# Window attention and a SiLU FFN on one core: block products for the second FFN product from the third chunk on, and a new order of operations

## The chip, the cores and the metric

The kernel runs on one core of a Trainium2 chip. The metric is the device time of one execution in microseconds (us). An execution has five engines with their own instruction streams: TensorE (PE in the profile; its weight loads are PEld), VectorE (DVE), ScalarE (ACT), GpSimdE (POOL) and SyncE (SP), which issues the DMA transfers.

## The reference

Four sequences of 768 positions with 8 heads of 64 go through an attention with a window of 15 positions to either side, plus 24 block summaries (the maximum of 32 keys, the mean of 32 values). The result, 3072 tokens of 512 numbers, goes through an FFN with a SiLU gate.

```python
k_sum = k.reshape(B, H, nb, block, D).max(axis=3)
v_sum = v.reshape(B, H, nb, block, D).mean(axis=3)
scores_l = where(|i - j| < 16, scale * q @ k^T, -1e9)
scores_s = scale * q @ k_sum^T + log(block)
a = softmax([scores_l, scores_s])
x = (a @ [v, v_sum]) as (3072, 512)
h = x @ w_in                       # 512 -> 2048
out = (h * sigmoid(h)) @ w_out     # 2048 -> 512
```

## The kernel before

**Tiling.** The attention runs in 24 stages of 128 positions: scores on TensorE (`job_scores`), softmax on VectorE, ScalarE and GpSimdE (`job_a`), values (`job_c`), and the result as x (`job_x`, L756 and L757). Two stages fill one chunk of 256 tokens, and the FFN takes the 12 chunks in turn. Attention for chunk c + 2 is put among the FFN of chunk c; three x buffers stand in a ring.

**The FFN.** Its 2048 inner columns are 16 blocks of 128; a unit is a pair of blocks (chunk 0 also has two single ones), so a chunk has 8 units. Each unit has a first product (x by w_in, into a PSUM bank of 512 columns), the gate (tanh on ScalarE, then one VectorE operation, which makes t), and a second product that accumulates over the chunk's units in PSUM. Chunk 0 works in f32. From chunk 1 on every operand is a sum of a high and a low f16 half, and a product is three f16 passes: high by high, high by low, low by high.

**Two forms of the second product.** `job_f` (L839 on) splits t into two halves (L889, L890) and multiplies directly: for two blocks, two halves of the 256 rows and three passes, 12 matmuls of 512 columns (L874), into two banks; at the chunk's end two copies (L911, L912) scale them into the output. `job_fast` (L952 on) treats the unit as a 2 by 2 matrix of blocks by another, and forms seven block products instead of eight (Winograd's form of Strassen's method): it splits three blocks of t (L969, L970), makes four sums of blocks in three subtractions on GpSimdE or VectorE (L974; the first is twice as wide), splits these (L976, L977), and issues seven products of three passes, 21 matmuls of 256 columns (L989), into four banks. At the chunk's end one copy and four VectorE additions (L1014, L1018, L1019) put the output together. The matching sums of w_out blocks are made once for each pair of blocks by `job_quad` (L929 to L934), ahead of the first use, and kept.

**What decides the form, and when the weight sums are made:**

```python
g, rest = divmod(i - FAST * NFT + EARLY, PACE)                            # L1161
if 0 <= g < NFT // 2 and not rest:                                        # L1162
    job_quad(g, n, FAST * NFT + 2 * g - TUNE["quad"])                     # L1163
(job_f if c < FAST else job_tail if c == NCHUNK - 1 and closes else job_fast)(n, c, fs)   # L1164
```

Here i counts blocks over all chunks (16 to a chunk, NFT = 16), and PACE is 4.

**The order of the work.** Every operation is recorded with its inputs, outputs and the engines that could run it (`Plan.op`). Two constants then settle the program: `RANKS` gives each operation a priority, and `ENGINES` a letter for its engine (P TensorE, D a DMA from SyncE, V VectorE, A ScalarE, G GpSimdE). A list scheduler (`Plan.sweep`, L124 on) takes the operations by them with assumed durations, and fixes each engine's own order; on the chip an engine follows its order and waits for its inputs. Where the scheduler foresees TensorE waiting in the first part, it puts fill matmuls on the identity (L310), whose result nobody reads.

**The start.** The first keys (`job_k0`), the first queries (`job_qk`), the values for the block means (`job_mean`) and the weights (`job_load`) come in as DMA transfers. The scores of the first two stages run in two halves each, the second when the third and fourth part of k have landed and been reduced. Three steps of eight matmuls (L522) sum the values for the means.

Of the kernel before, what the change touches and what calls it, by code (L numbers as in the profile page):

```python
# [56 lines left out]
FAST = 3  # L57
EARLY = 32
# [147 lines left out]
def local_attn_ffn(ctx: ExitStack, tc: tile.TileContext, qkT, qP, qF, kF, v, vR, vP, w, out):  # L206
# [1151 lines left out]
```

## Time and profile before

| | us |
|---|---|
| median of 3 runs | 570.09 (569.42 to 570.16) |
| the profiled execution | 570.2 |
| its span, first to last instruction | 568.5 |
| TensorE busy in it | 560.2 (99%) |
| VectorE busy | 483.1 (85%) |
| ScalarE busy | 391.8 (69%) |
| GpSimdE busy | 154.0 (27%) |

The profile is that of one execution. A busy time is the union of an engine's instructions. Matmuls overlap in their pipeline, so the time from one start to the next tells more of their cost than their own length. The stretches in the rows below follow the chunks roughly: chunk 0 runs from 22 to 86 us, chunk 1 from 86 to 131, chunk 2 from 131 to 179, with its last products up to 190, and then one chunk every 41 to 46 us.

### The profile page before, as it was taken

The numbers are of one execution on the slowest core, as the hardware profiler recorded it, in microseconds if no ns is written. First come the engines' busy times: TensorE is split into PE (matmuls) and PEld (weight loads), VectorE is DVE, ScalarE is ACT, GpSimd is POOL, SyncE is SP. The second block draws the span as 40 slices with busy tenths as digits, with TensorE's granted clock in tenths as the row PEclk, the third lists the DMA queues.
The fourth block names the chain that finished last, engine by engine and source line by source line (L and its number), as shares of the span: only waits on it lengthen the run. The fifth ranks groups of instructions, "written<-read, shape, count | busy, mean of one in ns | idle before, by whom it ended". The sixth has DMA issues, their size and how long they took to land.

```text
span 568.5 us, 16089 instructions
## 1 busy us (share of the span) xinstructions
PE 560.2 (99%) x6428; PEld 456.0 (80%) x6428; DVE 483.1 (85%) x1213; ACT 391.8 (69%) x995; POOL 154.0 (27%) x241
## 2 busy tenths in 40 slices
PE   8999999999999999999999999999999999999997
PEld 4767657676666888888888888888888888888885
DVE  6999989998999988998989877999988967834646
ACT  4999979767768975667878685758846766534431
POOL 4301000452523124232302212331323423323410
PEclk9999999999999999999999999999999999999999
DMA  8999733333895667346774567374871329200101
GB/s 331 414 419 414 283 107 103 99 109 107 187 230 103 186 163 92 122 119 209 195 184 144 161 122 93 134 132 106 236 190 48 85 57 65 75 1 3 38 1 37
DMA packets 66736, 83.92 MB, mean 148 GB/s; under 512 B 44950, under 2 KB 45350, under 8 KB 64870
## 3 DMA queue, kind: packets, MB, share of 16 engines
q1 hardware_dynamic: 66662, 82.91, 53.5%
q8 instruction: 50, 0.82, 0.6%
q14 instruction: 24, 0.20, 0.1%
HBM read 61.60 MB, written 11.16 MB: 128 GB/s over the span
## 4 chain that ended last, share of the span: by engine, by line
PE 83%; DMA 7%; ACT 5%; DVE 4%; issue 1%; SPq 0%; DVEq 0%; ACTq 0%
PE bank L949 30%; PE bank L989 26%; PE bank L861 7%; PE bank L874 7%; DMA wr<-in_w_dram 4%; PE bank L871 3%; PE bank L739 3%; PE bank L858 2%; PE bank L611 2%; DMA raw<-in_vR_dram 1%; ACT e L650 1%; ACT wr L786 1%; PE bank L724 1%; DMA first<-in_kF_dram 1%; ACT wr L782 1%; DMA raw<-in_qF_dram 1%
## 5 line engine op out<-in xcount | busy, mean ns | idle before, releaser
L949 PE MATMUL bank<-x,wr 128*128 128x256 f16 x1728 | 202.8, 273 | 0.0
L949 PEld LDWEIGHTS <-wr 128*128 128x128 f16 x1728 | 168.4, 98 | 20.2
L989 PE MATMUL bank<-wr 128*128 128x256 f16 x1491 | 177.2, 273 | 0.1
L974 POOL TENSOR_TENSOR wr<-wr 128x256 f32<-128x256 f32 (+1 forms) x139 | 95.2, 685 | 246.0 <-DVE wr L965 143.9
L989 PEld LDWEIGHTS <-wr 128*128 128x128 f16 x1491 | 144.1, 98 | 18.6 <-issue 0.3
L964 ACT ACTIVATE wr<-bank,th 128x512 f32<-128x512 f32 x71 | 48.5, 683 | 49.2 <-PE bank L949 48.8
L650 ACT ACTIVATE e<-e,mx 128x120 f32<-128x120 f32 x192 | 73.1, 382 | 10.9 <-DVE mx L647 10.9
L965 DVE SCALAR_TENSOR_TENSOR wr<-wr,bank 128x512 f32<-128x512 f32 x71 | 48.5, 683 | 27.6 <-ACT wr L964 27.2
L976 ACT ACTIVATE wr<-wr 128x512 f16<-128x512 f32 x71 | 44.3, 625 | 38.8 <-POOL wr L974 25.9
L977 DVE SCALAR_TENSOR_TENSOR wr<-wr 128x512 f16<-128x512 f32 x71 | 50.3, 709 | 17.3 <-ACT wr L976 17.0
L969 ACT ACTIVATE wr<-wr 128x384 f16<-128x384 f32 x71 | 36.9, 520 | 33.3 <-DVE wr L965 32.8
L970 DVE SCALAR_TENSOR_TENSOR wr<-wr 128x384 f16<-128x384 f32 x71 | 43.1, 607 | 6.2 <-ACT wr L969 5.2
L861 PE MATMUL bank<-x,wr 128*128 128x256 f16 x384 | 45.4, 273 | 0.0
L647 DVE CUSTOM_DVE_ANT_0 e<-bank,masks,qsc 128x120 f32<-128x120 f32 x144 | 42.4, 336 | 3.2 <-PE bank L611 3.0
L861 PEld LDWEIGHTS <-wr 128*128 128x128 f16 x384 | 37.1, 98 | 8.1 <-issue 0.3
L650 ACT ACTIVATION_READ_ACCUMULATOR e<-e,mx 128x1 f32 x192 | 36.1, 188 | 0.0
L929 POOL TENSOR_TENSOR wr<-wr 128x256 f32<-128x256 f32 x25 | 22.3, 901 | 35.5 <-DVE wr L934 10.3
L871 PE MATMUL bank<-wr,work 128*128 128x512 f32 x64 | 30.1, 597 | 0.1
L858 PE MATMUL bank<-x,wr 128*128 128x256 f32 (+1 forms) x144 | 30.1, 359 | 0.0
L858 PEld LDWEIGHTS bank<-x,wr 128*128 128x128 f32 x144 | 24.8, 190 | 5.3 <-issue 2.2
L665 POOL TENSOR_SCALAR e<-e,sum 128x120 f32<-128x120 f32 x26 | 10.4, 410 | 63.5 <-ACT e L650 31.9
L974 DVE TENSOR_TENSOR wr<-wr 128x128 f32<-128x128 f32 (+1 forms) x74 | 24.3, 328 | 2.4 <-POOL wr L974 1.7
(174 smaller groups left out, 798.6 us busy)
## 6 DMA issues: line engine op xcount, KB each, us to landing
wr<-in_w_dram SPq DMA_DIRECT2D x14, 1024.0 KB
raw<-in_qkT_dram SPq DMA_DIRECT2D x18, 576.0 KB
out_dram<-raw SPq DMA_DIRECT2D x23, 256.0 KB
first<-vd SPq DMA_DIRECT2D x30, 192.0 KB
raw<-in_kF_dram SPq DMA_DIRECT2D x12, 384.0 KB
raw<-in_qF_dram SPq DMA_DIRECT2D x9, 512.0 KB
raw<-in_vR_dram SPq DMA_DIRECT2D x12, 384.0 KB
raw<-in_vP_dram SPq DMA_DIRECT2D x9, 512.0 KB
```

Of the source, the lines that this page charges most:

```text
L650: plan.op({"act": 385}, lambda e, i=i, j=j, et=et, mx=mx: nc.scalar.activation(out=et[:, i, :], in_=et[:, i, :], func=AF.Exp, scale=-1.0, ...
L858: nc.tensor.matmul(out=o, lhsT=wi[:, ct * P:(ct + 1) * P], rhs=x0[:, ct, cs], start=(ct == 0), stop=(ct == NCT - 1))
L861: nc.tensor.matmul(out=o, lhsT=wip[:, part, ct * P:(ct + 1) * P], rhs=x[:, ct, :], start=(ct == 0 and q == 0), stop=(ct == NCT - 1 and q = ...
L871: nc.tensor.matmul(out=bank[ob[u]], lhsT=t[:, rows], rhs=wo, start=begins, stop=stops)
L949: nc.tensor.matmul(out=h[:, at * CH:at * CH + CH], lhsT=wip[:, p, ct * P:(ct + 1) * P], rhs=x[:, ct, :], start=(ct == 0 and q == 0), stop= ...
L964: plan.op({"act": 573}, lambda e: nc.scalar.activation(out=t, in_=h, func=AF.Tanh, scale=th[:, 0:1]), r=bk(k) + [("th", b % 2), "areas"], ...
L965: plan.op({"dve": 604}, lambda e: nc.vector.scalar_tensor_tensor(out=t, in0=t, scalar=1.0, in1=h, op0=ALU.add, op1=ALU.mult), r=bk(k), w=t ...
L970: plan.op({"dve": 470}, lambda e: nc.vector.scalar_tensor_tensor(out=ld, in0=src, scalar=SHRINK, in1=hd, op0=ALU.mult, op1=ALU.subtract), ...
L974: plan.op({"pool": 135 + 290 * size, "dve": 213 if size == 1 else 459}, lambda e, o=o, x=x, y=y: eng[e].tensor_tensor(out=o, in0=x, in1=y, ...
L976: plan.op({"act": 540}, lambda e: nc.scalar.activation(out=hs, in_=sf, func=AF.Copy, scale=SHRINK), r=[("sm", j)], w=[("hs", j)], prio=post)
L977: plan.op({"dve": 610}, lambda e: nc.vector.scalar_tensor_tensor(out=ls, in0=sf, scalar=SHRINK, in1=hs, op0=ALU.mult, op1=ALU.subtract), r ...
L989: nc.tensor.matmul(out=acc_of(c, m)[0], lhsT=x[:, left[m]], rhs=right[m](p), start=(opens and q == 0 and m in (1, 4, 2, 7)), stop=(closes ...
```

## The change

`FAST` goes from 3 to 2, so that chunk 2 too goes through `job_fast`. `EARLY` goes from 32 to 16, so that FAST * NFT - EARLY stays 16 and the weight sums are still recorded with blocks 16, 20 to 44. `RANKS` and `ENGINES` are replaced as a whole.

```diff
-FAST = 3
-EARLY = 32
+FAST = 2
+EARLY = 16
...
 RANKS = (
-    85, 28, 79, 25, 68, 114, 74, 106, 92, 65, 117, 138, 153, 163, 154, 335, 378, 544, 526, 132, 112, 19, 23, 2, 5, 3, 204, 216, 311, 465, 370, 425, 509, 607, 729, 599, 69,
...
+    (2792 priorities in place of 2760)
...
 ENGINES = (
-    "GDVDVDVDVDDDDDDDDDDPPPAVGAVGAGAGGAGAPPVAVAVAVAAVAVAGGGPPVVV
...
+    "GDVDVDVDVDDDDDDDDDDPPPAVGAGGGGVGGVAVPPVAVAVAVAAVAVGGAGPPVAV
...
```

The letters of the two strings, counted; "chunk 2's own" is what the new form itself adds:

| | P | V | A | G | D |
|---|---|---|---|---|---|
| before | 552 | 1011 | 726 | 233 | 238 |
| after | 540 | 1016 | 753 | 245 | 238 |
| difference | -12 | +5 | +27 | +12 | 0 |
| of which chunk 2's own | -12 | +21 | +8 | +15 | 0 |
| of which operations in both | 0 | -16 | +19 | -3 | 0 |
| of these, up to the end of chunk 2's list | 0 | -5 | +13 | -8 | 0 |

The engines of the three subtractions in chunk 2's eight units, in order: GGG, GVV, GVG, VVV, GGG, GGV, VVG, GVG.

Priorities of some of the first operations, a lower one first:

| operation | before | after |
|---|---|---|
| transfers of k, parts 0 to 3 | 28, 25, 114, 106 | 2, 1, 6, 15 |
| transfers of v for the means, 0 to 2 | 117, 138, 153 | 8, 35, 44 |
| scores, first halves of stages 0 and 1 | 69, 76 | 7, 9 |
| sums for the means, 0 to 2 | 132, 112, 19 | 24, 56, 72 |
| first transposes of stage 0 | 104, 93 | 51, 39 |
| scores, second halves of stages 0 and 1 | 118, 131 | 42, 45 |

## Rows read from the trace of the kernel before

**Rows 1.** The page, part 1: busy us (share) and instructions of each engine.
```profile
PE 560.2 (99%) x6428; PEld 456.0 (80%) x6428; DVE 483.1 (85%) x1213; ACT 391.8 (69%) x995; POOL 154.0 (27%) x241
```

**Rows 2.** Table of stretches: length, busy us (instructions) by engine, TensorE clock, DMA.
```profile
22.00:86.00 64.00, 62.97 (x379) 42.70 (x375) 59.92 (x128) 59.95 (x125) 5.39 (x10) 1.00 0.79 315
86.00:132.00 46.00, 46.00 (x488) 33.17 (x487) 44.54 (x104) 35.71 (x84) 16.67 (x26) 1.00 0.36 106
132.00:178.00 46.00, 46.00 (x526) 31.02 (x524) 42.78 (x110) 36.36 (x99) 16.83 (x18) 1.00 0.64 159
178.00:226.00 48.00, 48.00 (x625) 40.71 (x623) 42.21 (x119) 35.84 (x91) 13.66 (x21) 1.00 0.75 149
226.00:268.00 42.00, 42.00 (x504) 37.07 (x502) 40.47 (x97) 28.26 (x76) 11.16 (x18) 1.00 0.50 150
268.00:310.00 42.00, 42.00 (x546) 37.15 (x545) 37.94 (x99) 33.01 (x91) 8.48 (x12) 1.00 0.68 176
...
352.00:394.00 42.00, 41.88 (x543) 36.76 (x541) 41.30 (x113) 28.87 (x78) 12.06 (x17) 1.00 0.51 113
```

**Rows 3.** Timeline: start us, length us, engine, line, tiles, shape, count; TensorE, two places.
```profile
173.55 5.35 PE L874 MATMUL bank<-wr 128*128 128x512 f16 x24
...
178.74 2.78 PE L949 MATMUL bank<-x,wr 128*128 128x256 f16 x24
...
547.27 2.46 PE L989 MATMUL bank<-wr 128*128 128x256 f16 x21
...
549.56 1.47 PE L949 MATMUL bank<-x,wr 128*128 128x256 f16 x12
```

**Rows 4.** Groups by line and shape: count | busy us, mean ns of one | idle before.
```profile
L989 PEld LDWEIGHTS <-wr 128*128 128x128 f16 x1491 | 144.1, 98 | 18.6 <-issue 0.3
...
L977 DVE SCALAR_TENSOR_TENSOR wr<-wr 128x512 f16<-128x512 f32 x71 | 50.3, 709 | 17.3 <-ACT wr L976 17.0
...
L969 ACT ACTIVATE wr<-wr 128x384 f16<-128x384 f32 x71 | 36.9, 520 | 33.3 <-DVE wr L965 32.8
...
L970 DVE SCALAR_TENSOR_TENSOR wr<-wr 128x384 f16<-128x384 f32 x71 | 43.1, 607 | 6.2 <-ACT wr L969 5.2
...
L974 DVE TENSOR_TENSOR wr<-wr 128x128 f32<-128x128 f32 x51 | 14.6, 286 | 2.1 <-POOL wr L974 1.7
...
L1014 DVE SCALAR_TENSOR_TENSOR raw<-bank,th,wr 128x512 f32<-128x512 f32 x18 | 13.4, 744 | 2.1 <-PE bank L989 2.0
...
L974 DVE TENSOR_TENSOR wr<-wr 128x256 f32<-128x256 f32 x23 | 9.7, 420 | 0.3
...
L890 DVE SCALAR_TENSOR_TENSOR wr<-wr 128x512 f16<-128x512 f32 x8 | 6.4, 797 | 0.1
...
L784 DVE TENSOR_SCALAR wr<-wr 128x1024 uint32<-128x1024 uint32 x7 | 4.9, 695 | 0.0
...
L1014 DVE SCALAR_TENSOR_TENSOR raw<-bank,th,wr 128x256 f32<-128x256 f32 x9 | 4.3, 475 | 0.0
...
L912 DVE TENSOR_SCALAR raw<-bank,th 128x512 f32<-128x512 f32 x1 | 0.7, 745 | 0.0
```

**Rows 5.** Timeline, 168 to 200 us: x, block products, weight sums.
```profile
174.91 0.69 DVE L757 SCALAR_TENSOR_TENSOR x<-bank,x 128x512 f16<-128x512 f32 x1 [0.21 <-ACT x L756]
...
190.05 1.15 PE L989 MATMUL bank<-wr 128*128 128x256 f16 x9
...
195.09 1.28 DVE L934 SCALAR_TENSOR_TENSOR wr<-wr,ws 128x1024 f16<-128x1024 f32 x1
```

**Rows 6.** Timeline of TensorE, 0 to 53 us; in brackets its idle time and releaser.
```profile
6.85 0.40 PE L614 MATMUL bank<-first,second 64*64 64x96 f32 x8 [1.29 <-DMA second<-in_qP_dram]
...
8.26 2.55 PE L310 MATMUL bank<-ident 128*128 128x512 bf16 x11
...
12.06 1.06 PE L522 MATMUL bank<-wr,sums 128*32 128x512 f32 x8
...
41.21 0.40 PE L614 MATMUL bank<-first,second 64*64 64x96 f32 x8 [0.78 <-DMA second<-in_qP_dram]
```

More of the change, by code (lines that the diff above doesn't have):

```diff
@@ L1184 @@
 RANKS = (
[92 rows of a table removed]
[93 rows of a table added]
 )
 ENGINES = (
-    "GDVDVDVDVDDDDDDDDDDPPPAVGAVGAGAGGAGAPPVAVAVAVAAVAVAGGGPPVVVAVAVAVAVVVVGGGGPPVAPPPPAPPVAVAVAVAAVAVGGGGPPAVVAVAVAVAAVAVAGAGPPAVPPPPVDPVAVAVAVAAVGAAAPVAVAVAVAVAVVA"
-    "GGVPAAPVVVVPVPVVVVVVVAVDPVAVAVAVAVVAGAGPAAVAVAVAVAAVGVAVPAAPAVDAAVVDAVVADAVVVDAVVADAVVVADAVVVVDAAVVVDAVVVADAAVVVDAAVVADAVVVADAAVVVDAVVVADAAVVVDAAVVADAVVVADAVVVV"
-    "DAAVVAVPVPVVVVVVVVAVAVAVAVAVVVVVAVAVAVAVAVAVAVAVAVPPAVPPPPAVPPPPAVPPPPPPAVPPPPPPAVPPPPPPAVPPPPPPAVPPPPPPAVPPPPPPAVPPPPADADDPVAVAVAVAVVGAAGPAVVAVAVAVAVVGAAAPVVDD"
@@ L1284 @@
-    "VADVADVADVADADADAVVVDVVVVVVVPVAVAVAVAAVGAAGPAVVAVAVAVAAVGAAGPVAPAVPAVGGGGGGGGGGGAVVVDAVAVADVVDVVDVVDVVVVDVVVVVVVVAVDDGDVVDDAVDDDPVAVAVAVAVVVAVDDVAVAVAVAVVGVVDDD"
-    "AVAVGDDGGGGVAVPPAVAVPPPPPPAVAVPPPPGGGGAVPPAVAVPPPPPPAVAVPPPPGGGGAVPPAVAVPPPPPVAVAVAVAAVVAVDDVAVAVAVAAVGAVDDPAVPPAVAVPPPPGGGGAVPPAVAVPPPPPPAVAVPPPPADADDAVVVADAVD"
-    "DPVAVAVAVAAVAAVDDVAVAVAVAAVAAVDDPAVDAVAVADGGGVAVPPAVAVPPPPPPAVAVPPPPVGVGVVPPAVAVPPPPPPAVAVPPPPVVGVAVPPAVAVPPPPPVAVAVAVAVVVAVDDVAVAVAVAAVVAVDDPAVPPAVAVPPPPGGGGAV"
@@ L1287 @@
-    "PPAVAVPPPPPPAVAVPPPPADVDDAVAVADDVADVADVADVADADADAVVVDVVVVVVVPVAVAVAVAAVVAVDDVAVAVAVAVVVVVDDPAVDVVVVADPPAVAVGGGAVPPPPPPAVAVGGGAVPPPPAVAVVVGAVPPPPAVAVGVVAVPPPPAVA"
-    "VGVGAVPPPVAVAVAVAAVAAVDDVAVAVAVAAVGAVDDPAVPPAVAVGVGAVPPPPAVAVGGGAVPPPPAVAVGVGAVPPPPGVVVVVDDAVVVDVVAVVDVVDVVDVVDVVVVDVVVVVVVVAVDDDVVDDAVDDDPVAVAVAVAAVAAVDDVAVAVA"
-    "VAAVAVVDDPAVDAVAVADDPPAVAVGGGAVPPPPPPAVAVGVGAVPPPPAVAVVGGAVPPPPAVAVGGGAVPPPPAVAVGGGAVPPPVAVAVAVAAVAAVDDVAVAVAVAAVAAVDDPAVPPAVAVGGGAVPPPPAVAVVVVAVPPPPAVAVGGGAVPP"
@@ L1290 @@
-    "PPGAVVVVDDDAVAVVDAVDDPVAVAVAVAAVVVVDDVAVAVAVAVVGVVDDPAVDAVAVGDPPAVAVGGGAVPPPPPPAVAVVGVAVPPPPAVAVGGVAVPPPPAVAVGGVAVPPPPAVAVVVVAVPPPVAVAVAVAVVGAVDDVAVAVAVAAVVAVDD"
-    "PAVPPAVAVVVGAVPPPPAVAVVVVAVPPPPAVAVGVVAVPPPPGAVVVVDDDAVVVADDVADVADVADVADADADAVVVDVVVVVVVPVAVAVAVAAVVAVDDVAVAVAVAAVAAVDDPAVDAVAVGDPPAVAVGVGAVPPPPPPAVAVGGGAVPPPPA"
-    "VAVVVVAVPPPPAVAVVVVAVPPPPAVAVGGGAVPPPVAVAVAVAAVAAVDDVAVAVAVAAVGAVDDPAVPPAVAVVVGAVPPPPAVAVGGGAVPPPPAVAVVGVAVPPPPGAVVVVDDAVVVDVVVVADVVDVVDVVDVVVVDVVVVVVVVAVDDDAVD"
@@ L1293 @@
-    "DAVDDDPVAVAVAVAVVVAVDDVAVAVAVAAVAVVDDPAVDAVAVADDPPAVAVGGGAVPPPPPPAVAVGGVAVPPPPAVAVVGVAVPPPPAVAVGGVAVPPPPAVAVVGGAVPPPVAVAVAVAAVAVVDDVAVAVAVAAVVVVDDPAVPPAVAVGGGAV"
-    "PPPPAVAVGVGAVPPPPAVAVVVGAVPPPPGAVVVVDDDAVAVVDAVDDPVAVAVAVAAVVAVDDVAVAVAVAVVGAVDDPAVDAVVVGDPPAVAVGVVAVPPPPPPAVAVGGGAVPPPPAVAVGGGAVPPPPAVAVGVVAVPPPPAVAVGGGAVPPPVA"
-    "VAVAVAAVAVVDDVAVAVAVAAVAVVDDPAVPPAVAVVVVAVPPPPAVAVGVGAVPPPPAVAVVGGAVPPPPGVVVVVDDDVVAVADPVAVAVAVAAVVVVDDVAVAVAVAAVGAVDDPAVDAVAVGDPPAVAVGGVAVPPPPPPAVAVGGGAVPPPPAV"
@@ L1296 @@
-    "AVGGGAVPPPPAVAVVGGAVPPPPAVAVGVVAVPPPVAVAVAVAAVAVVDDVAVAVAVAAVAAVDDPAVPPAVAVVGGAVPPPPAVAVGGGAVPPPPAVAVGVVAVPPPPGVVVVVDDPAVPPAVAVVVGAVPPPPPPAVAVGGGAVPPPPAVAVGGVAV"
-    "PPPPAVAVGGGAVPPPPAVAVGGGAVPPPPAVAVVGGAVPPPPAVAVVGGAVPPPPAVAVGGGAVPPPPGAVVVVDDPPAVAVGGGAVPPPPPPAVAVGGGAVPPPPAVAVGGGAVPPPPAVAVVVVAVPPPPAVAVGGVAVPPPPAVAVGVVAVPPPPA"
-    "VAVVGVAVPPPPGVVVVVGPPAVAVAVAVPPPPPVDVDVD"
+    "GDVDVDVDVDDDDDDDDDDPPPAVGAGGGGVGGVAVPPVAVAVAVAAVAVGGAGPPVAVAVAVAVAVVAVVVGGPPAVPPPPAPPVAVAVAVAAVAVGGGGPPVAVAVAVAVAVVVVGGAGPPAAPPPPADPVAVAVAVAVVGGGAPVVVAVAVAVAAVA"
@@ new lines @@
+    "GGGPAAPVVVVPVPVVVVVVVAVDPVAVAVAVAVVGVAGPAVVAVAVAVAVVGAAAPVVPAVDAAVVDAAVADAAVVDAVVVDAVVVADAVVVADAVVVVDAAVVVDAAVVVDAAVVADAAVVADAAVVADAAVVADAVVVADAVVVADAAVVADAVVVA"
+    "DAAVVAVPVPVVVVVVVVAVAVAVAVVVAVAVAVAVVVAVVVAVAVAVAVPPAVPPPPAVPPPPAVPPPPPPAVPPPPPPAVPPPPPPAVPPPPPPAVPPPPPPAVPPPPPPAVPPPPADADDPVAVAVAVAAVAAGAPVVVAVAVAVAAVAAAAPAADD"
+    "VADVADVADVADADADAVVVDVVVVVVVPVAVAVAVAAVAAVAPAAVAVAVAVAAVAAAVPAAPAVPAVGGGGGGGVVVGAVVVDAVAVADVVDVVDVVDVVVVDVVVVVVVVAVDDGDVVDDAVDDDPVAVAVAVAAVAAVDDVAVAVAVAAVAAVDDD"
@@ new lines @@
+    "AVAVADDGGGGGAVPPAVAVPPPPPPAVAVPPPPGGGVAVPPAVAVPPPPPPAVAVPPPPGGVGAVPPAVAVPPPPPVAVAVAVAAVAAVDDVAVAVAVAAVAAVDDPAVPPAVAVPPPPGVGGAVPPAVAVPPPPPPAVAVPPPPADVDDAVAVGDAVD"
+    "DPVAVAVAVAAVAAVDDVAVAVAVAVVAAVDDPAVDAVAVADGVGGVVPPAVAVGGGAVPPPPPPAVAVGVVAVPPGVVVAVPPAVAVGVGAVPPPPAVAVVVVAVPPGGGGAVPPAVAVGGGAVPPPVAVAVAVAVVGAVDDVAVAVAVAAVAAVDDPA"
+    "VPPAVAVGGVAVPPGVVGAVPPAVAVVVGAVPPPPAVAVGVGAVPPPPGAVVVVDDDAVAVADDVADVADVADVADADADAVVVDVVVVVVVPVAVAVAVAVVAAVDDVAVAVAVAVVVAVDDPAVDAVVVGDPPAVAVGVGAVPPPPPPAVAVGGVAVP"
@@ new lines @@
+    "PPPAVAVGVGAVPPPPAVAVGGGAVPPPPAVAVGGVAVPPPVAVAVAVAAVAAVDDVAVAVAVAAVAAVDDPAVPPAVAVGVVAVPPPPAVAVGGGAVPPPPAVAVVGGAVPPPPGVVVVVDDAVVVDAVAVADVVDVVDVVDVVVVDVVVVVVVVAVDD"
+    "DAVDDVVDDDPVAVAVAVAAVAAVDDVAVAVAVAAVAAVDDPAVDAVAVADDPPAVAVGGGAVPPPPPPAVAVGGGAVPPPPAVAVGVVAVPPPPAVAVGVGAVPPPPAVAVGGGAVPPPVAVAVAVAAVAVVDDVAVAVAVAVVAAVDDPAVPPAVAVG"
+    "VGAVPPPPAVAVVGGAVPPPPAVAVGVGAVPPPPGAVVVVDDDAVAVVDAVDDPVAVAVAVAAVAVVDDVAVAVAVAVVGVVDDPAVDAVAVVDPPAVAVGGGAVPPPPPPAVAVGGGAVPPPPAVAVVGGAVPPPPAVAVGVGAVPPPPAVAVVVGAVP"
@@ new lines @@
+    "PPVAVAVAVAAVGVVDDVAVAVAVAVVVAVDDPAVPPAVAVGGGAVPPPPAVAVGGGAVPPPPAVAVVGGAVPPPPGAVVVVDDDAVAVGDDVADVADVADVADADADAVVVDVVVVVVVPVAVAVAVAAVAAVDDVAVAVAVAVVVAVDDPAVDAVVVG"
+    "DPPAVAVGGGAVPPPPPPAVAVVGGAVPPPPAVAVGVGAVPPPPAVAVGGGAVPPPPAVAVVGGAVPPPVAVAVAVAAVAAVDDVAVAVAVAAVAAVDDPAVPPAVAVVGVAVPPPPAVAVGVVAVPPPPAVAVGVGAVPPPPGAVVVVDDAVVVDAVAV"
+    "ADVVDVVDVVDVVVVDVVVVVVVVAVDDDAVDDAVDDDPVAVAVAVAAVAAVDDVAVAVAVAAVAAVDDPAVDAVAVADDPPAVAVGGGAVPPPPPPAVAVGGGAVPPPPAVAVVVVAVPPPPAVAVGGVAVPPPPAVAVGGVAVPPPVAVAVAVAAVVA"
@@ new lines @@
+    "VDDVAVAVAVAVVGAVDDPAVPPAVAVGGGAVPPPPAVAVGGVAVPPPPAVAVVVVAVPPPPGAVVVVDDDAVAVVDAVDDPVAVAVAVAAVGAVDDVAVAVAVAAVVAVDDPAVDVVAVGDPPAVAVGGGAVPPPPPPAVAVGGGAVPPPPAVAVGGVA"
+    "VPPPPAVAVGGVAVPPPPAVAVVGVAVPPPVAVAVAVAAVAAVDDVAVAVAVAAVGAVDDPAVPPAVAVGVVAVPPPPAVAVGVVAVPPPPAVAVGGVAVPPPPGAVVVVDDDVVAVVDPVAVAVAVAAVVVVDDVAVAVAVAAVVVVDDPAVDVVAVAD"
+    "PPAVAVVGGAVPPPPPPAVAVGGGAVPPPPAVAVVGGAVPPPPAVAVVGGAVPPPPAVAVGVGAVPPPVAVAVAVAVVVVVDDVAVAVAVAAVAVVDDPAVPPAVAVGVGAVPPPPAVAVGGGAVPPPPAVAVVGGAVPPPPGAVVVVDDPAVPPAVAVG"
@@ L1299 @@
+    "GGAVPPPPPPAVAVVGGAVPPPPAVAVVGVAVPPPPAVAVGGGAVPPPPAVAVVGGAVPPPPAVAVGGVAVPPPPAVAVGGGAVPPPPAVAVVGGAVPPPPGAVVVVDDPPAVAVGVVAVPPPPPPAVAVVGVAVPPPPAVAVVGGAVPPPPAVAVGGGA"
+    "VPPPPAVAVGGVAVPPPPAVAVVGVAVPPPPAVAVVVVAVPPPPGAVVVVGPPAVAVAVAVPPPPPVDVDVD"
 )
```

184 rows, old and new, of the table RANKS are left out of this document.

## The prediction

> **What bounds the kernel now.** I read the page's busy shares first, then the table of stretches, then the order of the matmuls. TensorE is busy for 560.2 of the 568.5 us span at a granted clock of 1.00, the upper level of 2.4 GHz [rows 1, 2]. The reader should not stop there, since a pipelined engine can look busy and be slow; so the start-to-start times matter. 24 matmuls of 512 columns take from 173.55 to 178.74, 216 ns each; 21 of 256 columns take from 547.27 to 549.56, 109 ns each [rows 3]. From 86 us on TensorE has no idle time to speak of: none in the five stretches to 310, 0.12 us from 352 to 394 [rows 2]. So there the kernel is as long as TensorE's list of work: work taken off it there is time won, as long as the other engines can still feed it.
>
> The engine to watch is VectorE. In the stretches 86 to 132, 132 to 178 and 178 to 226 it is busy for 44.54, 42.78 and 42.21 us, 129.53 of 140 [rows 2]. It has 10.5 us left there; ScalarE and GpSimdE have far more (9.6 and 29.2 us in 132 to 178 alone).
>
> **The change, part by part.**
>
> *Products (removed from the path).* A unit is a pair of FFN blocks. In chunk 2 a unit's second product is now 12 matmuls of 512 columns (two blocks, two halves of the rows, three half-precision passes), and becomes 21 of 256 (seven block products, three passes). By rows 3 that is 12 x 216 = 2.595 us against 21 x 109 = 2.290 us, 0.305 us less; eight units: **-2.44 us**. The first product (24 x 109 ns) is untouched. This term lies wholly on the path.
>
> The trace's row and a rule differ here. In the row, wide matmuls in a stream stand 216 ns apart [rows 3]. The Trainium skill, "TensorE: Matmul & The Clock Gate", section "Back-to-back issue gap", says that a sustained stream of weight loads and matmuls runs at about 131 ns per matmul of 512 columns and about 81 ns per matmul of 128. By that rule twelve wide ones would cost 1.57 us and 21 of 256 columns at least 1.70, and this term would be a loss of at least 1 us (rival E). The trace does not agree with the rule's 131 ns.
>
> *Block sums (added, beside the path).* For each unit VectorE now forms two low halves (607 and 709 ns) in place of one (797): +0.52 us, eight times 4.15 [rows 4]. The subtractions of a unit stand in the new engine string as GGG, GVV, GVG, VVV, GGG, GGV, VVG, GVG: two double ones (420 ns) and eight single ones (286) on VectorE, 3.13 us; six double and eight single ones go to GpSimdE, which is idle for most of that time [rows 2, 4]. Closing the chunk costs four additions (three of 744, one of 475) in place of one copy of 745: 1.96 us. **VectorE +9.2 us.** ScalarE gets one more copy of 384 columns per unit, 8 x 0.52 = 4.2 us, inside its 9.6 idle.
>
> *Shared weight sums (moved).* The eight "quad" jobs exist already and are issued beside the same units as before (48 - 32 = 32 - 16). But their user is now chunk 2, and the last one ends at 196.4 now [rows 5]. It has to be ready before the last unit of chunk 2, near 180. So the last two, with 1.28 us of VectorE each [rows 5] plus their sums, move forward by some 15 us; their total is unchanged.
>
> *Does VectorE still keep up?* The place that decides is the start of chunk 3. Its second half of x is written at 174.91 to 175.60, and its first matmul starts at 178.74: 3.1 us of lead [rows 3, 5]. By then VectorE must do most of the new work: 9.2 less the closing additions, 7.3, and about 2.6 for the two quads, so 9.9 us more. Cover: 4.7 us idle from 86 to 178 and 4.1 from 22 to 86 [rows 2]. The engine strings give the rest: among the operations that stand in both, 16 net leave VectorE, but only five of these belong to the parts up to the list of chunk 2; at between 0.29 (a block subtraction) and 0.70 us (a weight shift) each [rows 4], 1.4 to 3.5 us. 4.7 + 4.1 + 2.4 = 11.2 against 9.9: it fits, with nearly every idle slot used. An idle slot is not always usable, because each operation has its own inputs to wait for, so I book a stall of TensorE of **+0.5 us**, between 0 and 5.2 (9.9 - 4.7, if only the near idle time and no move helps). After 226 VectorE is 96 and 90% busy [rows 2], so what slips past chunk 3 is absorbed only slowly, but eleven of the sixteen operations leave it there.
>
> *Boundaries.* Accumulators: the seven products use four banks, and two of these hold chunk 1's sums until they are copied out. Today the same change of layout lies between chunks 2 and 3, the first block products start at 190.05 and TensorE has no gap around them [rows 2, 5]. Moved by a chunk it should cost nothing again; without that cover, one copy of 0.745 us [rows 4]. That sits in the bounds.
>
> *The new order (moved, everywhere).* From 86 us on there is no gap for it to close. Gaps and idle fills (matmuls on the identity that compute nothing) lie at the start: 11 fills from 8.26 to 10.74 while the second half of the first scores waits, and 0.78 us idle before 41.21 for a transfer of q; the first 6.85 us end with a transfer that nothing can pull forward [rows 6]. So at most 2.5 + 0.8 = 3.3 us are to be had. The new ranks move the first of the three sums for the block means, and one transpose, ahead of the second score halves, thus into the fills. Eight of the 24 matmuls of these sums, one such step, take 1.06 us [rows 6]. Against that, the last quarter of k is now issued behind the first transfer of v, so the second halves can come later. Bounds: 3.3 gained to 0.8 lost (one such wait as at 41.21). I take **-0.8 us**, a little under that row. The end has the same operations and is booked at nothing; it has no cover, and half a microsecond either way lies in the range.
>
> **Sum**, against the profiled execution of 570.2 us (span 568.5 and 1.7 around it): -2.44 + 0.5 - 0.8 = -2.7, so 567.5; the median of the runs is 0.1 lower, so **567.4 us**.
>
> **The rivals.**
>
> A. *VectorE is full, and slower.* One mechanism, at the start of chunk 3: if the operations moved off VectorE do not free it in time, 9.9 us of work meet 4.7 of idle time; x is 5.2 us late, and if the lead of 3.1 us is needed as it is now, TensorE waits all of it: -2.44 + 5.2 = +2.8, about 573. It turns slower once TensorE's waits exceed 2.4 us. For it: 97% busy in 86 to 132, 93% in 132 to 178. Against it: the engine string moves work away, and TensorE has products of older units to do while x is late (24 wide matmuls stood ready at 173.55 [rows 3]). Chance 0.07.
>
> B. *VectorE is nearly full, and the gain is eaten.* The lead is used up and 2.1 us (5.2 - 3.1) remain as waits, in one place or spread over the chunk: -2.44 + 2.1 = -0.3, about 569.8. Chance 0.14.
>
> C. *The start gains in full.* The fills and the wait for q vanish (-3.3) and nothing stalls: -5.7, 564.4; half of that start and no stall gives about 566. For it: the ranks of the first hundred operations are wholly new. Against it: the fills end on transfers and reductions that are still needed. Chance of 565.5 or below: 0.14.
>
> D. *The change does not do what it says*: the last quads come late, so that the last units' products wait and chunk 3's first products run first. TensorE would have chunk 3's first matmuls as filler, so the price is one quad's low half, 1.28 us [rows 5], and the time 568.7. Chance 0.06.
>
> E. *More and narrower matmuls cost more than they save.* Nine more matmuls per unit bring nine more weight loads of 98 ns [rows 4]. Were these not hidden behind the matmuls, a unit would grow by 9 x 98 - 305 = 577 ns, eight by 4.6 us: 574.5 with the other terms at nothing. Against it: the 109 ns of rows 3 hold with a weight load for each matmul. Chance 0.01. The rule of the Trainium skill named above ("Back-to-back issue gap") points the same way, to about 571.2.
>
> **How the numbers follow.** The forecast (565.5 to 568.6) has 0.58, C 0.14, D 0.06, B 0.14, A 0.07, E 0.01. About 0.2% (1.1 us) is what a measurement of this kernel can tell from no change. Faster by more than that, below 568.95: forecast, C and D, 0.78. Within it: B and a small part of A (0.01), 0.15. Slower, above 571.2: the rest of A and E, 0.07. The range reaches into C and B and leaves about one in ten out on either side: 565.2 to 569.9.
>
> **What would show it.** Right: 1659 block products (79 units x 21) and 96 wide matmuls; TensorE as good as without idle time from 86 us on; the first matmul of chunk 3 about 3 us earlier; VectorE at 97% or more between 86 and 226; fewer than 11 fills before the second score halves. Wrong: waits of TensorE's weight loads on VectorE's x or low halves between 130 and 230 (A, B), products waiting for the weight sums near 180 (D), or the second score halves starting later than 10.74 (the start lost).

## The result and the profile after

**Slower, not faster.** The median after the change is 576.3 us against 569.9 of the kernel before, run on the same chip: ratio 1.012 (1.010 to 1.014). I had forecast 567.4, with 569.9 as the upper end of the range. The execution profiled below took 576.5 us, its span is 574.4.

The table of stretches of the kernel after stands against [rows 2] (columns as there; the first number after the length is TensorE's busy time):

```profile
22.00:53.00 31.00, 31.00 (x249) 22.70 (x250) 30.05 (x85) 30.51 (x72) 4.54 (x10) 1.00 1.02 416
53.00:86.00 33.00, 31.86 (x163) 20.77 (x159) 32.29 (x52) 31.48 (x53) 1.35 (x3) 1.00 0.60 220
86.00:132.00 46.00, 45.15 (x451) 30.80 (x450) 43.01 (x99) 36.34 (x92) 15.28 (x21) 1.00 0.32 96
132.00:178.00 46.00, 44.22 (x596) 36.72 (x591) 42.69 (x123) 38.77 (x109) 15.48 (x21) 1.00 0.67 168
178.00:226.00 48.00, 48.00 (x640) 42.22 (x638) 42.67 (x110) 40.34 (x109) 17.46 (x22) 1.00 0.75 150
226.00:268.00 42.00, 41.67 (x501) 36.76 (x499) 40.02 (x106) 31.00 (x88) 12.64 (x18) 1.00 0.48 138
...
352.00:394.00 42.00, 39.85 (x468) 34.19 (x466) 36.04 (x95) 28.45 (x85) 9.73 (x16) 0.96 0.59 130
```

Before, TensorE had no idle time between 86 and 520 us but 0.12. Now it idles 0.85, 1.78, 0.33 and 2.15 us in four stretches, and 1.14 between 53 and 86. In the last row the mean granted clock is 0.96. The waits of TensorE's matmuls in the kernel after (line, what it waited for: us in total, times, longest):

```profile
PE bank L989 <- DVE wr L970: 2.2, 1, 2.2
PE bank L739 <- DMA first<-vd: 1.8, 2, 1.3
...
PE bank L522 <- DMA wr<-in_vP_dram: 0.8, 1, 0.8
PE bank L871 <- DVE wr L813: 0.7, 1, 0.7
```

These are not one place but many: a low half of the block products at 357 us, the values of window 6 at 160, the first values at 15, halves of the weights at 83. The groups by line and shape of the kernel after, against [rows 4], show that the products themselves arrived as meant, 79 units of 21 and 8 units of 12:

```profile
L989 PE MATMUL bank<-wr 128*128 128x256 f16 x1659 | 199.2, 273 | 2.5 <-DVE wr L970 2.2 <-DVE raw L1014 0.3
...
L874 PE MATMUL bank<-wr,work 128*128 128x512 f16 x96 | 22.7, 379 | 0.0
```

**The largest loss, followed back.** The timeline of TensorE in the kernel after:

```profile
355.25 0.38 PE L989 MATMUL bank<-wr 128*128 128x256 f16 x2
357.78 0.39 PE L989 MATMUL bank<-wr 128*128 128x256 f16 x1 [2.15 <-DVE wr L970]
357.97 5.24 PE L949 MATMUL bank<-x,wr 128*128 128x256 f16 x32
```

It waits 2.15 us for a low half of the block products. And the 32 matmuls behind the wait take 5.24 us. At the spacing of [rows 3] they would take 2.78 + 8 x 0.109 = 3.65. Right behind the idle time the granted clock is 0.50, the lower level of 1.2 GHz (columns as in the table of stretches), and that is another 1.6 us:

```profile
357.78:361.19 3.41, 3.41 (x17) 2.41 (x18) 3.41 (x18) 2.70 (x12) 0.45 (x1) 0.50 0.26 56
```

Not every execution has such a fall. Of the six, the three with a granted clock of 0.996 over the whole, this one among them, took 576.5 to 579.0 us, and the three with 0.999 to 1.000 took 575.8 to 576.1. So the loss stands without the fall too. What was the low half late for? VectorE's timeline there:

```profile
350.02 0.68 DVE L977 SCALAR_TENSOR_TENSOR wr<-wr 128x512 f16<-128x512 f32 x1
356.30 0.95 DVE L450 TENSOR_REDUCE am<-raw 128x1 f32<-128x768 f32 x1 [5.60 <-DMA raw<-in_vR_dram]
357.17 0.55 DVE L970 SCALAR_TENSOR_TENSOR wr<-wr 128x384 f16<-128x384 f32 x1
```

VectorE stood still for 5.6 us, because the next operation in its fixed order, a maximum over values of the fourth sequence (L450), waited for their transfer. The low half (L970) is queued behind it and needed nothing that was late. The issues of SyncE tell what the transfer stood behind:

```profile
343.32 0.88 SPq L580 DMA_DIRECT2D first<-vd  x2
344.30 5.05 SPq L706 DMA_TRANSPOSE third<-first  x2
349.52 0.47 SPq L447 DMA_DIRECT2D raw<-in_vR_dram  x1
```

The DMA row and the rate in GB/s for 340 to 358 us, in 40 slices of 0.45 us, of the kernel after:

```profile
DMA  8710000860957990909000000000990089990000
GB/s 328 193 24 0 0 0 0 164 128 9 218 205 167 127 32 23 28 28 32 27 23 27 27 23 27 27 23 18 288 78 3 10 271 328 295 215 0 0 0 0
```

From the 15th slice to the 28th, 346.3 to 352.6 us, only 18 to 32 GB/s move. The second transfer of L580 (158 KB: 79 rows of 2 KB, the second half of the values of a sequence's last window) trickles through. 158 KB at 25 GB/s are 6.3 us, the length of that trough. The trace's packet records show it: of the 175 packets of 2 KB of the two halves, 101 start between 344.49 and 346.34 us (as many as the 96 rows of the first half and five more), and the other 74 follow one at a time, one every 80 ns, until 352.28. What is issued meanwhile lands behind it: the load of L447 at 356.3, 6.8 us after its issue, where 3 to 3.5 are usual (one issued at 106.15 is read from 109.49 on). The Trainium skill, "DMA: Bandwidth & Descriptors", section "Why a DMA increments its semaphore by 16 and not by 1", has the rule: a copy is spread over the largest number of engines, up to 16, that divides its slowest dimension on both sides. 79 is prime, which by that rule leaves one engine, while 96 and 64 get 16. The trace agrees: 74 packets one at a time here, against 101 in 1.85 us just before. The kernel before has the same transfer and the same trough; VectorE's waits there, 340 to 356 us:

```profile
DVE am L450 <- DMA raw<-in_vR_dram: 2.7, 1, 2.7
```

There TensorE has no idle time between 310 and 352 us: nothing that it needed soon was queued behind L450.

### The profile page after: what moved, and what is told of

The parts are those of the page before. It is cut to its first block, busy times and chain, and to the rows that moved or that the text cites. A ratio compares the mean times of both kernels' runs of the same rounds, so it can differ in the third digit from the quotient of the medians.

```text
span 574.4 us, 16306 instructions
## 1 busy us (share of the span) xinstructions
PE 560.5 (98%) x6495; PEld 462.7 (81%) x6495; DVE 486.6 (85%) x1218; ACT 407.5 (71%) x1045; POOL 161.7 (28%) x252
## 4 chain that ended last, share of the span: by engine, by line
PE 73%; DMA 11%; DVE 9%; ACT 4%; issue 2%; SPq 1%; POOL 0%; DVEq 0%; ACTq 0%
PE bank L949 35%; PE bank L989 30%; DMA wr<-in_w_dram 5%; PE bank L739 3%; PE bank L611 2%; DMA raw<-in_vR_dram 2%; DMA wr<-in_vP_dram 2%; DMA raw<-in_qF_dram 2%; DVE wr L814 1%; DMA first<-vd 1%; DVE e L647 1%; ACT wr L812 1%; PE bank L874 1%; DVE wr L788 1%; DVE wr L934 1%
## 5 line engine op out<-in xcount | busy, mean ns | idle before, releaser
L989 PE MATMUL bank<-wr 128*128 128x256 f16 x1659 | 199.2, 273 | 2.5 <-DVE wr L970 2.2
L974 POOL TENSOR_TENSOR wr<-wr 128x128 f32<-128x128 f32 (+1 forms) x160 | 111.4, 696 | 289.4 <-DVE wr L965 157.3
L964 ACT ACTIVATE wr<-bank,th 128x512 f32<-128x512 f32 x79 | 53.7, 680 | 47.7 <-PE bank L949 47.4
L965 DVE SCALAR_TENSOR_TENSOR wr<-wr,bank 128x512 f32<-128x512 f32 x79 | 53.8, 681 | 31.1 <-ACT wr L964 30.6
L976 ACT ACTIVATE wr<-wr 128x512 f16<-128x512 f32 x79 | 49.3, 624 | 38.2 <-POOL wr L974 28.4
L977 DVE SCALAR_TENSOR_TENSOR wr<-wr 128x512 f16<-128x512 f32 x79 | 55.9, 708 | 12.9 <-ACT wr L976 12.4
L969 ACT ACTIVATE wr<-wr 128x384 f16<-128x384 f32 x79 | 41.0, 519 | 30.1 <-DVE wr L965 29.8
L970 DVE SCALAR_TENSOR_TENSOR wr<-wr 128x384 f16<-128x384 f32 x79 | 50.0, 633 | 10.4 <-ACT wr L969 9.7
L663 ACT ACTIVATE e<-e,sum 128x120 f32<-128x120 f32 x109 | 34.3, 383 | 0.6 <-DVE sum L658 0.6
L703 DVE TENSOR_TENSOR first<-e,first 128x480 f16<-128x480 f32 x36 | 24.9, 695 | 0.1
```

What stands on the lines that cost most here:

```text
L964: plan.op({"act": 573}, lambda e: nc.scalar.activation(out=t, in_=h, func=AF.Tanh, scale=th[:, 0:1]), r=bk(k) + [("th", b % 2), "areas"], ...
L965: plan.op({"dve": 604}, lambda e: nc.vector.scalar_tensor_tensor(out=t, in0=t, scalar=1.0, in1=h, op0=ALU.add, op1=ALU.mult), r=bk(k), w=t ...
L969: plan.op({"act": 430}, lambda e: nc.scalar.activation(out=hd, in_=src, func=AF.Copy, scale=SHRINK), r=tks, w=[("hd", j)], prio=post)
L970: plan.op({"dve": 470}, lambda e: nc.vector.scalar_tensor_tensor(out=ld, in0=src, scalar=SHRINK, in1=hd, op0=ALU.mult, op1=ALU.subtract), ...
L974: plan.op({"pool": 135 + 290 * size, "dve": 213 if size == 1 else 459}, lambda e, o=o, x=x, y=y: eng[e].tensor_tensor(out=o, in0=x, in1=y, ...
L976: plan.op({"act": 540}, lambda e: nc.scalar.activation(out=hs, in_=sf, func=AF.Copy, scale=SHRINK), r=[("sm", j)], w=[("hs", j)], prio=post)
```

## The experiments

Two theories at first. **Theory 1:** the new order, laid out for assumed durations, puts in-order engines behind transfers and sums that come later than planned. **Theory 2:** the block products in chunk 2 overfill VectorE.

| kernel | TensorE idle 0-53 | 53-132 | 132-178 | 178-268 | 352-394 | ratio to before (95%) |
|---|---|---|---|---|---|---|
| before | 4.13 | 0 | 0 | 0 | 0.12 | 1 |
| after | 3.72 | 1.99 | 1.78 | 0.33 | 2.15 | 1.012 (1.010 to 1.014) |
| order_alone | 4.42 | 1.25 | 0.14 | 1.45 | 2.53 | 1.012 (1.009 to 1.015) |
| products_alone | 3.11 | 2.41 | 0 | 2.51 | 0 | 1.005 (1.003 to 1.007) |
| after_split | 4.66 | 1.59 | 2.30 | 0 | 0 | 1.005 (1.003 to 1.007) |
| before_split | 4.05 | 0 | 0 | 0 | 0 | 1.000 (0.998 to 1.001) |
| after_light | 3.82 | 1.53 | 1.29 | 0 | 0 | 1.004 (1.002 to 1.005) |
| after_early6 | 4.54 | 1.42 | 1.78 | 1.36 | 0 | 1.007 (1.005 to 1.009) |
| told | 3.78 | 2.97 | 1.26 | 3.20 | 0 | 1.014 (1.010 to 1.017) |
| start_alone | 3.73 | 0.36 | 0 | 0 | 0.17 | 0.999 (0.998 to 1.001) |
| old_loads | 3.73 | 1.61 | 0.10 | 0 | 0 | 1.000 (0.999 to 1.001) |
| start_told | 4.74 | 2.13 | 0.45 | 0.46 | 0 | 1.003 (1.002 to 1.005) |
| loads_light | 3.89 | 1.01 | 0.10 | 0 | 0 | 0.999 (0.998 to 1.000) |
| before_light | 3.20 | 0 | 0 | 0 | 0.21 | 0.999 (0.998 to 1.000) |

Idle us are a stretch's length less TensorE's busy time in the one profiled execution, added up from tables of stretches like the one above; the ratios are over all executions.

**order_alone and products_alone: the two halves of the change, each by itself.** Constants: `FAST = 3`, `EARLY = 32` with the new `RANKS` and `ENGINES` of the operations that stand in both; and `FAST = 2`, `EARLY = 16` with the old ones. Neither is pure: order_alone's ranks were mended by hand between 125 and 400 us, so there its order is a new one, but not that of the changed kernel; and in the trace of products_alone VectorE's order is that of the kernel before only up to 60 us and after 282.

> The kernel before (chunk 2 by wide products) in the new order: every operation that stands in both kernels takes its place and its engine from the changed kernel; between 125 and 400 us ranks were mended by hand until the planner's own forecast had no hole (it forecasts 568.3 against 567.9 for the old order). Theory 1, the new order loses the time (in-order engines stand behind transfers and sums that come later than the planner assumed): slower than before by 3 to 8 us, 573 to 578, with waits of TensorE near 15, 54 to 90, 130, 160 and 350 us as in the changed kernel. Theory 2, the block products in chunk 2 lose it (VectorE is too full): 569.5 to 571, no new waits but those before 53 us.

> The changed kernel (chunk 2 by seven block products, weight sums 16 blocks earlier) in the old order: before 84 us and after 230 us ranks and engines of the kernel before, the new ones between, and there mended until the planner's forecast had no hole over 0.9 us (567.3 against 567.9 for before and 565.8 for the changed kernel). Theory 1 (the order): 568 to 571, the chunks from 4 on at their old distances, the products' 2.4 us partly to be seen. Theory 2 (the products): 574 to 577, like the changed kernel, with TensorE's waits between 86 and 230.

A new order alone cost 1.2%, as much as the whole change, without a single new block product (577.3 us). Theory 1 had forecast that, and theory 2 no change. Its waits are of the same kinds: between 70 and 90 us on the weights, at 239 and at 364. TensorE in order_alone:

```profile
237.27 0.82 PE L989 MATMUL bank<-wr 128*128 128x256 f16 x6
239.54 1.47 PE L989 MATMUL bank<-wr 128*128 128x256 f16 x12 [1.45 <-DVE raw L1014]
...
364.56 0.28 PE L989 MATMUL bank<-wr 128*128 128x256 f16 x1 [1.90 <-DVE wr L977]
```

Both of these can be followed back to a load that lands behind 79 rows, as in the changed kernel. VectorE waits for it and then works without a pause until TensorE's wait ends:

```profile
226.67 0.95 DVE L448 TENSOR_REDUCE vm<-raw 128x24 f32<-128x768 f32 x1 [3.20 <-DMA raw<-in_vR_dram]
...
357.97 0.95 DVE L450 TENSOR_REDUCE am<-raw 128x1 f32<-128x768 f32 x1 [4.82 <-DMA raw<-in_vR_dram]
```

The products in the mostly old order cost 0.5% (573.5), between the two forecasts. TensorE in products_alone:

```profile
84.74 1.55 PE L871 MATMUL bank<-wr,work 128*128 128x512 f32 x3 [1.40 <-ACT wr L812]
...
229.06 0.28 PE L989 MATMUL bank<-wr 128*128 128x256 f16 x1 [1.25 <-DVE wr L977]
...
234.48 0.49 PE L989 MATMUL bank<-wr 128*128 128x256 f16 x3 [1.21 <-DVE wr L1019]
```

The releasers are ScalarE once and VectorE twice, which looks like theory 2. But the two waits for VectorE, 2.5 us, can be followed back to the 79 rows once more:

```profile
227.38 0.95 DVE L448 TENSOR_REDUCE vm<-raw 128x24 f32<-128x768 f32 x1 [5.06 <-DMA raw<-in_vR_dram]
...
228.31 0.69 DVE L977 SCALAR_TENSOR_TENSOR wr<-wr 128x512 f16<-128x512 f32 x1
```

The load was issued at 218.20, while 79 rows were under way, and VectorE stood still for 5.06 us before it. It was not short of room; it was held up and then behind, without a pause until 234. What is left for theory 2 is the 1.4 us for a half of the weights at 84.74. No run divides the 79 rows in this kernel or in order_alone, so the price of the products in an order like the old one, and that of the order without the late transfers, were not measured.

**after_split and before_split: the 79 rows in two transfers.**

```diff
-                nc.sync.dma_start(out=vv[at:at + hi - lo, z], in_=vd_t[b - 1][lo:hi])
+                for r, q in ((lo, lo + HALF), (lo + HALF, hi)) if t == NTILE - 1 and z else ((lo, hi),):
+                    nc.sync.dma_start(out=vv[at + r - lo:at + q - lo, z], in_=vd_t[b - 1][r:q])
```

> The changed kernel with one thing taken away: the last window's second half of values, 79 rows of 2 KB, is loaded as 64 and 15 rows in two transfers (three times in the run). In the trace these 79 packets go one behind the other, one per 84 ns, and everything issued after them lands late (landings of 9.5 and 6.8 us where 3 to 4 are usual). If these 79 rows are what delays the load of values' sums at 349.5, and with it the low half and TensorE at 357.8: that load lands in 3 to 4 us, the 5.6 us wait of VectorE and the 2.3 us wait of TensorE go, and with them the 1.8 us of matmuls at half clock: 572.2 to 574. If the transposes ahead of it are what delays it: the landing stays above 6 us and the time at 576 +- 0.7.

> The same division of the 79-row transfer in the kernel before. There TensorE does not wait near 350, so the time should stay (569.5 to 570.5) while VectorE's 2.7 us wait near 350 goes and the transfers near 216, 342 and 470 land in 3 to 5 us. A gain of over 1 us would say that the late transfers cost the kernel before too.

573.2 instead of 576.3 us, in an unchanged order. In the profiled execution the late load now lands in 3.6 us, TensorE's wait at 357 and the fall of the clock behind it are gone (idle 0 in 352 to 394), and the trough with them: all 175 packets of the two halves pass between 344.57 and 346.52. Other executions still have a fall somewhere: five of ten, with a granted clock of 0.993 to 0.997 over the whole, took 573.6 to 575.7 us. The rate in after_split, same window and slices:

```profile
GB/s 348 217 31 0 0 0 0 119 171 1 73 328 282 105 133 195 9 144 131 10 7 0 116 82 273 371 262 61 0 0 0 0 0 0 0 18 84 55 266 375
```

That is shown, then: three transfers of 79 rows, together with the order that put a low half behind them, were 3 to 4 us of the loss (by medians and by ratios). The transposes ahead of the load, the rival, are still there, and TensorE waits for nothing behind them. In the kernel before the same division changes nothing: its order had no use for what it freed.

**after_light: less VectorE work in chunk 2.** In after_split, `part = slice(0, 16) if c == 2 and f > 5 else slice(None)` on both low halves (L970, L977).

> The changed kernel with the 79 rows in two transfers, where VectorE forms the two low halves of chunk 2's last five units on 16 columns only instead of 384 and 512 (the rest of these halves is left out), same order: some 4.5 us less for VectorE between 145 and 180, in the very sums that the change adds. Theory 2 (this work is what delays the rest): the wait of 2.4 us for values near 160 and what comes after it shrink, 569.5 to 571.5. Theory 1 (late transfers): VectorE idles more, the wait near 160 stays over 1.5 us, and the time stays at 572.5 to 573.8.

572.0 us; VectorE's busy time between 132 and 178 fell from 43.12 to 40.06 us, the idle time of TensorE there from 2.30 to 1.29. But in the changed kernel, whose order is the same up to there, that idle time was 1.78, so half a microsecond of the 1.0 can be chance. Some of the wait goes with VectorE's work, and 1.29 us stays with the transfers. The intervals of the two ratios overlap, so the time itself decides nothing; the wait lies between the theories.

**after_early6: window 6's values issued earlier.** Two of SyncE's issues are moved, all else word for word as in after_split.

> The changed kernel with the 79 rows in two transfers, and on SyncE two issues moved: the means of window 6 go in three transposes earlier (near 148.5 instead of 152), and its values one transpose earlier (near 153 instead of 154.5). TensorE, VectorE, ScalarE and GpSimdE keep their order word for word. Theory 1 (TensorE stands behind late transfers): the wait of 2.4 us near 160 falls to 0.5 to 1.3, 571.5 to 572.5. If the values land at the same time because other transfers fill the queues: no change, 573.2 +- 0.5.

A miss: 574.0 us, not to be told from the 573.2 of after_split (the intervals of the ratios overlap). TensorE in after_early6:

```profile
159.63 0.97 PE L740 MATMUL bank<-third,first 120*64 120x64 f16 x48 [1.26 <-DMA third<-first]
...
178.66 0.27 PE L950 MATMUL bank<-x,wr 128*128 128x256 f16 x1 [1.13 <-ACT x L757]
```

The values were there, but now the transpose that had been moved behind them was late, and x of chunk 3 after it. Between 147 and 171 us SyncE issues one transfer behind another, and here moving one passed the wait on.

**told: a planner that knows of late transfers.** The planner is told that transfers land 0.5 to 2 us later than it had assumed, and the order is searched again.

> The changed kernel with the 79 rows in two transfers, and with a planner that is told what the traces show of the transfers: to each transfer's landing it adds 0.5 us (transposes, the first loads) to 0.7 us (q, k, values) or 2.0 us (windows' values), and ranks and engines were searched again with that. Its forecast, on purpose a late one, is 570.9 (the old order, told the same and not searched again: 580). Theory 1 (the order stands behind transfers that come later than planned): 566.5 to 570, no single wait of TensorE after 22 us over 1 us but the planned ones near 136 and 178. Theory 2 (VectorE has no room for chunk 2's block sums): 572 or more, TensorE waits for VectorE's halves and x between 86 and 240 whatever the order.

The clearest miss of theory 1: 578.0 us, slower than the change itself. After 22 us the transfers' waits did go but for 0.7 us at 179, and new ones for VectorE and ScalarE came (1.7 us for halves of the weights at 91, 2.5 us for a low half at 182). That is what theory 2 had forecast, 572 or more. So theory 1 in its narrow form, "it is the transfers", falls. A wider form fits the orders tried here, but is argued and not shown: an order fitted to a forecast without reserve meets waits in places that the forecast doesn't have, and whether the cause is a transfer or a queue of sums differs from place to place.

**start_alone: the start, by itself.** The new order before 60 us only.

> The kernel before, with places and engines of the changed kernel only for the operations before 60 us. This measures the term that the prediction booked at -0.8 (bounds -3.3 to +0.8). The planner's forecast is 567.4 against 567.9, so -0.5. If the moved block means wait for the first values (1.2 us in the changed kernel): 569.5 to 571, no gain; if they fill the idle fills as the prediction had it: 568.5 to 569.5.

570.0 us, ratio 0.999 (0.998 to 1.001): no gain that can be measured. That is the range given for sums that wait for the first values, but the profiled execution shows no such wait, so the reason stays open.

**old_loads and start_told: the mended version, two ways.**

> The changed kernel with the 79 rows in two transfers, window 6 advanced as in the run beside it, and the old order for what starts before 15 us (the first loads of values again ahead of the weights, the first block-mean sum again after the second score halves); ranks between 20 and 200 us searched again. The planner forecasts 567.2, where it forecasts 567.9 for the kernel before and 565.8 for the changed one. Theory 1: nothing waits at 15.5, so the waits of the weights' halves near 70 to 90 shrink too (VectorE and ScalarE are no longer 0.9 us behind their plan from 16 us on): 568.5 to 570.5, chunk 1 at 85 or before. Theory 2 (VectorE has no room between 53 and 86 with this order, whatever the start): TensorE still loses 1.5 us or more between 53 and 132, 571 to 573.

> As the run beside it, but with the new order of the first loads kept and the places before 200 us searched again with the late landings of the first values and of window 6's values (0.3 to 0.7 and 1.5 us later) told to the planner; it forecasts 567.3. Theory 1: as before or a little better, 568.5 to 571. Theory 2: 571 to 574.

old_loads takes 570.4 us where the kernel before takes 570.4, ratio 1.000 (0.999 to 1.001). With the old order of the first loads, the 79 rows divided, window 6 issued earlier and the places before 200 us searched again, all of the loss is won back, and no more. How much each of these did besides the 79 rows is not shown. The time lies in theory 1's range; the 1.61 us that TensorE still loses between 53 and 132 are what theory 2 had forecast. start_told, with the new first loads, takes 572.1 us (1.003), in the range that theory 2 gave it. Stretches of old_loads:

```profile
53.00:86.00 33.00, 31.98 (x173) 20.76 (x169) 31.95 (x52) 30.91 (x52) 1.57 (x3) 1.00 0.59 216
86.00:132.00 46.00, 45.41 (x458) 31.31 (x457) 43.60 (x99) 36.94 (x92) 15.28 (x21) 1.00 0.32 96
132.00:178.00 46.00, 45.90 (x611) 38.05 (x608) 45.65 (x127) 41.58 (x117) 19.19 (x23) 1.00 0.66 171
```

VectorE is busy for 45.65 of 46 us in 132 to 178, and TensorE idles only 0.10 there. A full VectorE alone does not stop TensorE. But between 53 and 132 it still idles 1.61 us, at 71, 83, 89 and 131, and a pause costs more than it shows as idle: a matmul reads 273 ns long where the next starts 109 after it. By an estimate from these numbers, 1.61 + 4 x 0.16 = 2.3 us, that is about what the products won.

**loads_light and before_light: are VectorE and ScalarE what is left?** In `job_k`, `few = 2 if b == 1 else BLK` keys of each block are read.

> The mended version with the old first loads (570.4, as fast as the kernel before), where VectorE's key maxima and ScalarE's key sums of the second sequence (three of their four parts stand between 62 and 73 us) read 2 keys of each block of 32, the rest is left out; same order. This gives VectorE some 2.3 us and ScalarE some 2.2 us just ahead of the waits that are left: 0.6 us at 71 for the bound of the weights, 0.75 and 0.5 at 83 and 89 for halves of the weights. If the fullness of these two engines between 53 and 86 is what now eats the products' 2.4 us: the three waits go, chunk 1 starts about 1 us earlier, 568.3 to 569.3. If these waits lie elsewhere (transfers, the order itself): 570.0 to 570.8.

> The control: the same part left out of the kernel before, which has no wait of TensorE in these places. Expected by every theory: 569.6 to 570.6, no change.

569.6 and, as the control, 570.2 us: ratios 0.9989 and 0.9988 to the kernel before, the same to within 0.1%. 569.6 lies between the two forecasts. The wait at 71 went (idle 53 to 86 fell from 1.02 to 0.41), that at 83 fell from 0.6 to 0.4, that at 89 stayed at 0.3, and the end did not move more than the control's. What holds those two is not settled.

The trace has a hint, argued and not shown. The low halves of w_in and w_out (L814, 16 of 1.28 us) are formed in the kernel after between 75 and 105 us; in the kernel before they run from 79 to 130. VectorE in the kernel before:

```profile
101.87 1.27 DVE L814 SCALAR_TENSOR_TENSOR wr<-wr,ws 128x1024 f16<-128x1024 f32 x1
...
114.21 1.28 DVE L814 SCALAR_TENSOR_TENSOR wr<-wr,ws 128x1024 f16<-128x1024 f32 x1
116.27 1.28 DVE L814 SCALAR_TENSOR_TENSOR wr<-wr,ws 128x1024 f16<-128x1024 f32 x1
...
128.57 1.28 DVE L814 SCALAR_TENSOR_TENSOR wr<-wr,ws 128x1024 f16<-128x1024 f32 x1
```

The weight sums of chunk 2 are wanted 16 blocks earlier, and everything that VectorE and ScalarE owe the weights moves forward with them, to where both were nearly full already (32.29 and 31.48 of 33 us in 53 to 86). The other runs fit: in order_alone, which has no new products, and in products_alone the same halves run from 77 to 107 us, and TensorE waits for halves of the weights between 83 and 90 in both; in start_alone they run from 78 to 130, and it waits for none.

## Why the prediction was wrong

*Products, -2.44 us: right as far as the traces go.* The counts are the forecast ones, and no run contradicts 109 ns a piece. No run measured the term by itself.

*VectorE at the start of chunk 3, +0.5: wrong place.* x was written from 177.41 to 178.07 and chunk 3 began at 178.33, so the lead shrank from 3.1 to 0.3 us, but TensorE did not wait for it. I had looked for the bottleneck where the new sums are formed. VectorE was not fuller there: it was busy for 128.37 of 140 us between 86 and 226, 92%, where I had given 97% as the sign of being right. Its and ScalarE's waits came earlier, at 71 to 89, 1.45 us in three places where the work on the weights was pulled to. I had counted 4.1 us of VectorE's idle time between 22 and 86 as cover; it is just that stretch.

*Boundary of accumulators, 0 (bound 0.745):* held. TensorE does not wait for a copy between chunks 1 and 2; one wait of 0.3 us on L1014 comes later, at 237.

*The start, -0.8:* no gain (start_alone, -0.3 with -1.1 to +0.5). The moved sum did take the place of fills (7 instead of 11 before the second score halves). But those halves began at 11.41 instead of 10.74, the sign I had named for a start that is lost, and a later sum waits 0.8 us for its values at 15.5.

**The step that failed is "The new order (moved, everywhere)": "From 86 us on there is no gap for it to close."** That is true, and I took it to mean that the order is worth nothing from 86 us on. But an order can open gaps as well as close them. I bounded the term by what the trace of before had to give, 3.3 us, and on the other side by one wait like that at 41.21, 0.8, in the start alone. The runs put it at about +7 in place of -0.8: order_alone, 577.3 against 570.2, with an order that differs in part from the changed kernel's; what the sum below puts down to order and transfers comes to 9. In [rows 2] the stretches at 100% are no proof of slack: they don't say how early each input was there, and every hand-over between the engines was laid anew. Nothing in my working priced that: the range had no term for it, and the rivals A, B and D look at chunks 2 and 3 alone.

**How the 6.8 us add up** (6.4 by the medians), by ratios of 570 us: -2.4 for the products (durations), +3.9 for the 79 rows and what follows from them (1.012 less 1.005), +3.0 for the first loads, window 6 and the places before 200 us (1.005 less 1.000), and 2.3 that remain in old_loads, which equal the products' gain. The last is a remainder, not a measurement.

*The rivals.* B (the gain is eaten, 569.8) comes near the mended version's 570.4 by luck, since the place was another. A did not happen: VectorE was busy for 42.69 of 46 us between 132 and 178, as before (42.78), and chunk 3's x came just in time. C, D and E did not happen: no wait on a weight sum shows, and matmuls of 256 columns kept their spacing. (E's own sum gives 574.7 and not 574.5; nothing hangs on it.) What I listed as a sign of failure, waits on low halves between 130 and 230, came at 357 instead.

## What to carry to other kernels

When a change comes with a new order of a program that runs at 100%, price the order as a risk and not as a chance. Take each in-order engine and ask what stands behind every wait on a transfer, as the 5.6 us of L450 held up a low half that needed nothing. And look at the row counts of the transfers: here three transfers of 79 rows cost 3 to 4 us, more than the 2.4 that the arithmetic could win, and nothing at all in the order that did not queue behind them. A wait that is charged to a busy engine can be a transfer's: step back on that engine to its own last idle time, as at 227.38 in products_alone.

## What the runs showed of the hardware

A transfer of 79 rows of 2 KB moved at 18 to 32 GB/s for 6 us, one packet every 80 ns, after 101 packets of it and its neighbour of 96 rows had gone through in 1.85, and a load issued behind it landed after 6.8 us instead of 3 to 3.5. Divided into 64 and 15 rows, all 175 rows went through in 1.95 us and the load landed in 3.6. After 2.15 us of idle time in a stretch that had been busy throughout, 32 matmuls took 5.24 us where 3.65 are usual, at a granted clock of 0.50 until 361.19: in that execution a wait of 2 us cost nearly 4. Three of the six executions show no such fall.
